# One loop in place of three on the path not taken, and its last stores on another queue

## Chip, cores and metric

The kernel runs on one core of a Trainium2 chip. The metric is the device time of one execution in microseconds, taken as the median of several runs. Besides, one execution was recorded by the profiler; all rows below are from it.

## What is computed

For each of 4 batches and 8 heads a gated linear attention runs over 768 time steps with a state of 48 x 48; its output, put together to 384 channels, goes through a causal convolution of 5 taps whose sigmoid gates a projection, and through a second projection:

```
for t in range(S):
    state = f[:, :, t, :, None] * state + einsum('bhd,bhe->bhde', k[:, :, t], v[:, :, t])
    y[:, :, t] = einsum('bhd,bhde->bhe', q[:, :, t], state)
...
gate = sigmoid(sum(conv_w[k] * xp[:, k:k + S] for k in range(5)))
out = (gate * (x @ w_val)) @ w_out
```

Here f is the sigmoid of the input f_logit, x is y with the heads side by side, and xp is x with four zero rows ahead of it.

## The kernel before

The kernel holds the computation twice. The **main path** (everything up to line 825) works in six chunks of 128 time steps. Within a chunk the recurrence becomes products of matrices, with running products of f factored into q and k. The order in which the five engines get their work is written out by hand in PROGRAM, a list of some hundreds of pieces; wrapped engines (class Ordered) keep that order. The chunked form is good only if the running products of f stay within a range. So the pieces rcheck, rcount and rflag form one number from the range test of all chunks, and the last of them writes `bad`.

At line 826 `values_load` brings `bad` into a register of each engine, and line 828 branches:

```
flag = nc.values_load(bad[:], min_val=0, max_val=1)
main.close()
with tc.If(flag == 0, preferred_fallthrough_block=False, label="good") as good:
    pass
with good.Else(), ExitStack() as sub:
    general(sub)
```

With a good flag nothing is left to do, and each engine jumps over the code of the **general path** (`general`, lines 636 to 711) to the closing barrier (line 883 of the builder). The general path would do the whole computation step by step with a scan: a nest of loops over the pairs of heads (two batch pairs `n`, four head pairs `i`, and `odd`; line 658) with an inner loop over the 48 rows of the state (line 675), and then a loop over the six chunks for convolution and projections (line 690). With the inputs of this kernel the flag is good, so none of it is executed; it only lies between the branch and the branch's target in each engine's instructions. SyncE issues the loads of q, f and k in it, ScalarE those of v and of the convolution's input and the stores of the pairs' results and of the outputs (lines 668, 689, 693, 711).

The pieces `hint 0` to `hint 4` (line 763) put one branch hint on each engine some time ahead of the branch, at places written in PROGRAM.

SyncE issues all stores of the main path (`send`, line 780); the last two pieces of its list are `send 6 2`, behind ScalarE's last copy, and the read of the flag.

The compiled program of the kernel before has 64 bytes for each instruction. Counted in it, labels of branch targets included (26 on each engine in this stretch), from the branch of line 828 to the first instruction of its target:

```
engine     instructions from branch to target     to the end of the program behind it
SyncE      221                                     22
ScalarE    193                                     6
VectorE    180                                     6
GpSimd     133                                     8
TensorE    274                                     6
```

## Time and profile before

| | |
|---|---|
| median of 3 runs | 191.07 us (191.02 to 191.68) |
| the profiled execution | 192.9 us |
| its span, first to last recorded instruction | 191.2 us |
| instructions recorded | 7637 |
| busy: TensorE, VectorE, ScalarE, GpSimd | 90%, 83%, 77%, 17% |
| last computing instruction ends | 184.7 us |

The profiled execution is 1.8 us above the median of the others; times within it are counted from the start of its span. The page's busy shares are means over the whole span. Register, branch, semaphore and DMA-issuing instructions are not counted as busy, so the stretch behind 184.7 us, in which there is nothing else, shows up in the page only as the zeros at the end of its slices. It is read from the instructions by line of the source: line 826 is the flag's read, line 828 the branch and the first instructions at its target, line 883 the closing barrier. In such rows "first and last start" is the place in time; a letter q behind an engine's name marks what its sequencer does itself (PEldq is TensorE's).

### The profile page before, as it was taken

What the parts mean: (1) busy time and instruction counts of PE and PEld (TensorE: products, weight loads), DVE (VectorE), ACT (ScalarE), POOL (GpSimd) and SP (SyncE); (2) the same over time, 40 slices, a digit from 0 to 9 for tenths busy, and PEclk for the clock granted to TensorE, in tenths of its full rate; (3) what the DMA queues carried; (4) which work ended last, traced back from release to release, by engine and by line L of the source; (5) the groups of instructions that cost most, each with busy time, mean ns of one, the idle gap of its engine ahead of it and who ended that gap; (6) DMA issues with size and microseconds to landing.
All of it is one profiled execution on the core that took longest, in us unless ns stands there. A gap on an engine that the chain in (4) does not pass through costs nothing.

```text
span 191.2 us, 7637 instructions
## 1 busy us (share of the span) xinstructions
PE 171.3 (90%) x3357; PEld 141.3 (74%) x3357; DVE 159.0 (83%) x236; ACT 146.9 (77%) x260; POOL 31.8 (17%) x57
## 2 busy tenths in 40 slices
PE   5478999996996899998999999989999999999960
PEld 1377878374885688887888887868878778898950
DVE  4069899999899999999999998999988989877000
ACT  8399799998775998987999999957357694575420
POOL 8300230088353300210000301200200000000000
PEclk9997999999999999999999999999999999999995
DMA  4997888887079648356389980620600010211430
GB/s 125 349 398 256 295 292 308 290 269 285 15 271 313 205 156 285 100 175 209 127 279 299 299 265 36 161 93 5 206 3 3 7 55 0 110 56 57 165 118 7
DMA packets 13064, 33.21 MB, mean 174 GB/s; under 512 B 1632, under 2 KB 3680, under 8 KB 13024
## 3 DMA queue, kind: packets, MB, share of 16 engines
q1 hardware_dynamic: 13024, 32.66, 50.5%
q8 instruction: 27, 0.44, 1.0%
q14 instruction: 13, 0.11, 0.2%
HBM read 26.75 MB, written 4.72 MB: 165 GB/s over the span
## 4 chain that ended last, share of the span: by engine, by line
PE 52%; DVE 22%; ACT 8%; DMA 6%; issue 4%; POOL 4%; SPq 1%; DVEq 0%
PE psum L127 52%; DVE kb L127 4%; DVE gt L127 4%; ACT e L127 4%; POOL wvL L127 4%; DMA qb<-in_q 3%; DVE qb L127 3%; DMA e<-in_f 3%; DVE e L127 2%; DVE asb L127 2%; DVE xL L127 2%; DVE ca L127 2%; DVE cb L127 1%; ACT ksb L127 1%; ACT xf L127 1%
## 5 line engine op out<-in xcount | busy, mean ns | idle before, releaser
L127 ACT ACTIVATE e<-e 128x1024 f32<-128x1024 f32 (+2 forms) x54 | 50.3, 942 | 3.6 <-DMA e<-in_f 3.0
L127 DVE SCALAR_TENSOR_TENSOR gt<-xf,cws,gt 128x512 f32<-128x512 f32 x48 | 37.4, 804 | 0.3 <-ACT gt L127 0.2
L127 PE MATMUL psum<-rg,woH 128*128 128x512 f32 (+1 forms) x108 | 32.1, 382 | 0.2 <-issue 0.2
L127 PE MATMUL psum<-asb,vb 64*32 64x64 f32 (+3 forms) x1152 | 27.5, 246 | 0.5 <-issue 0.4
L127 PEld LDWEIGHTS psum<-asb,vb 64*32 64x32 f32 (+1 forms) x1152 | 23.5, 115 | 1.7 <-issue 0.8
L127 DVE TENSOR_TENSOR_SCAN e<-keep,e 128x1024 f32<-128x1024 bf16 x10 | 23.9, 2386 | 0.0
L127 PE MATMUL psum<-qb,kb 64*64 64x128 f32 (+1 forms) x768 | 19.8, 250 | 2.8 <-DVE qb L127 2.4
L127 PEld LDWEIGHTS psum<-rg,woH 128*128 128x128 f32 x108 | 19.2, 188 | 3.8
L127 ACT CAST rg<-psum 128x512 fp32r<-128x512 f32 x30 | 17.1, 601 | 5.9 <-DVE psum L127 3.1
L127 PEld LDWEIGHTS psum<-qb,kb 64*64 64x64 f32 x768 | 17.9, 136 | 4.8 <-DVE qb L127 3.1
L127 PE MATMUL psum<-rg,woL 128*128 128x512 f32 (+1 forms) x54 | 20.3, 376 | 0.0
L127 PE MATMUL psum<-xH,wvL 128*128 128x512 f32 x45 | 17.9, 398 | 1.6 <-POOL wvL L127 1.6
L127 PE MATMUL psum<-xH,wvH 128*128 128x512 f32 x45 | 18.6, 414 | 0.6 <-DVE asb L127 0.5
L127 PE MATMUL psum<-qb,st 64*32 64x128 f32 (+1 forms) x480 | 19.1, 282 | 0.0
L127 PE MATMUL psum<-xL,wvH 128*128 128x512 f32 x45 | 17.8, 396 | 0.8 <-DVE xL L127 0.8
L127 DVE TENSOR_TENSOR kb<-kb,e 128x512 f32<-128x512 f32 (+1 forms) x28 | 17.2, 655 | 0.6 <-ACT e L127 0.6
L127 DVE TENSOR_TENSOR qb<-qb,e 128x1024 f32<-128x1024 f32 (+1 forms) x14 | 15.7, 1122 | 0.8 <-DMA qb<-in_q 0.8
L127 DVE TENSOR_TENSOR asb<-psum,tri 128x512 f32<-128x512 f32 x24 | 16.2, 681 | 0.0
L127 ACT COPY osb<-psum 128x512 f32<-128x512 f32 x15 | 8.6, 594 | 6.6 <-PE psum L127 6.5
L127 POOL TENSOR_TENSOR st<-u,e 128x384 f32<-128x384 f32 x8 | 9.2, 1157 | 26.0 <-DVE u L127 11.1
L127 PE MATMUL psum<-vb,ksb 128*64 128x48 f32 x320 | 11.6, 225 | 1.7 <-ACT ksb L127 1.7
L127 ACT COPY xf<-psum 128x768 f32<-128x768 f32 x12 | 9.6, 813 | 4.4 <-PE psum L127 4.4
(92 smaller groups left out, 309.0 us busy)
## 6 DMA issues: line engine op xcount, KB each, us to landing
e<-in_f SPq DMA_DIRECT2D x10, 512.0 KB, 5.7
kb<-in_k SPq DMA_DIRECT2D x10, 512.0 KB, 5.0
qb<-in_q SPq DMA_DIRECT2D x10, 512.0 KB, 5.2
vb<-in_v SPq DMA_DIRECT2D x10, 448.0 KB, 4.7
out<-osb SPq DMA_DIRECT2D x15, 256.0 KB, 3.7
raww<-in_wv SPq DMA_DIRECT2D x3, 384.0 KB, 4.9
raww<-in_wo SPq DMA_DIRECT2D x3, 384.0 KB, 5.8
e<-in_f SPq DMA_DIRECT2D x4, 256.0 KB, 4.6
```

Source lines behind the costliest of these rows:

```text
L127: ins = emit(*a, **kw)
```

## The change

The three loops over n, i and odd become one loop over all 16 pairs, and the indices are recovered from its counter by remainder and division. The three stores at the end of the loop over chunks are issued by SyncE instead of ScalarE. The main path is not edited.

```
-        with tc.For_i(0, 2, 1) as n, tc.For_i(0, NP, 1) as i, tc.For_i(0, 2, 1) as odd:
-            p = i * 2 + odd
-            bp = n * (2 * NP) + p
-            n1 = bass.ds(n, 1)
+        with tc.For_i(0, B * NP, 1) as bp:
+            p, odd = bp % (2 * NP), bp % 2
+            n1 = bass.ds(bp // (2 * NP), 1)
...
-                nc.scalar.dma_start(out[bass.ds(c, 1), :, o].rearrange("u p b t -> (u p) (b t)"), buf)
+                nc.sync.dma_start(out[bass.ds(c, 1), :, o].rearrange("u p b t -> (u p) (b t)"), buf)
```

## Rows read from the trace of the kernel before

**Rows 1.** The page's DMA queues: packets, MB, share of 16 engines' span.

```profile
q14 instruction: 13, 0.11, 0.2%
```

**Rows 2.** Busy time by stretch: PE, PEld, DVE, ACT, POOL, clock, DMA share, GB/s.

```profile
184.70:191.20 6.50, 0.00 (x0) 0.00 (x0) 0.00 (x0) 0.00 (x0) 0.00 (x0) 0.69 0.10 32
```

**Rows 3.** Line 828: operation, count, ns min/median/max, first and last start.

```profile
L828 SPq EVENT_SEMAPHORE  x8: 17/17/17, 189.3 to 189.8; - x8
L828 ACTq COMPARE_BRANCH  x1: 68/68/68, 184.9 to 184.9; - x1
L828 POOLq COMPARE_BRANCH  x1: 65/65/65, 184.9 to 184.9; - x1
L828 PEldq COMPARE_BRANCH  x1: 385/385/385, 185.0 to 185.0; - x1
L828 DVEq COMPARE_BRANCH  x1: 84/84/84, 185.0 to 185.0; - x1
L828 PEldq EVENT_SEMAPHORE  x1: 51/51/51, 185.4 to 185.4; - x1
L828 SPq COMPARE_BRANCH  x1: 70/70/70, 185.8 to 185.8; - x1
L828 ACTq EVENT_SEMAPHORE  x1: 17/17/17, 188.1 to 188.1; - x1
L828 DVEq EVENT_SEMAPHORE  x1: 21/21/21, 188.9 to 188.9; - x1
```

**Rows 4.** Line 883: the closing barrier, and the first of five hints.

```profile
L883 POOLq DRAIN  x3: 39/82/106, 185.4 to 190.9; - x3
L883 SPq DRAIN  x3: 7/7/7, 190.4 to 190.7; - x3
...
L883 POOLq BRANCH_PREFETCH_HINT  x1: 46/46/46, 147.1 to 147.1; - x1
```

**Rows 5.** SyncE's waits from 180 us: us in total, times, longest.

```profile
SPq L828 <- SPq L828: 3.4, 1, 3.4
```

**Rows 6.** DMA issues from 183 us: count, KB each, median us to landing.

```profile
out<-kb SPq DMA_DIRECT2D x2, 128.0 KB, 1.7
```

**Rows 7.** Instruction packets: 131 to 185.5, 185.9 to 186.1, 187.0 to 187.2, 188.7 to 189.9 us.

```profile
q8 instruction: 6, 0.10, 0.9%
...
q14 instruction: 3, 0.02, 36.0%
...
q14 instruction: 1, 0.01, 9.6%
...
q14 instruction: 3, 0.02, 6.4%
```

**Rows 8.** Instruction packets: 71.8 to 72.0 us, then 129.1 to 129.3 us.

```profile
q14 instruction: 1, 0.01, 17.2%
...
q14 instruction: 1, 0.01, 12.5%
```

**Rows 9.** Timeline of SyncE near 70 us: start, us, what.

```profile
70.20 0.42 SPq L127 DMA_DIRECT2D vb<-in_v  x1
```

**Rows 10.** SyncE's main line, 70.7 to 185.9 us: three of nine rows.

```profile
L127 SPq EVENT_SEMAPHORE  x34: 17/17/4687, 73.4 to 183.8; - x34
...
L127 SPq DMA_DIRECT2D out<-kb x6: 332/333/405, 179.2 to 184.5; - x6
...
L127 SPq DMA_DIRECT2D e<-in_f x2: 328/355/382, 91.5 to 101.8; - x2
```

**Rows 11.** ScalarE's main line, 107.2 to 185.0 us: first and last of 18.

```profile
L127 ACT CAST rg<-psum x18: 581/596/652, 113.8 to 168.5; 128x512 fp32r<-128x512 f32 x18
...
L127 ACT ACTIVATION_READ_ACCUMULATOR e<-e x1: 188/188/188, 113.4 to 113.4; 128x1 f32 x1
```

**Rows 12.** VectorE's main line, 128.2 to 185.1 us: first and last of 19.

```profile
L127 DVE SCALAR_TENSOR_TENSOR e<-xf,cws,e x24: 472/479/486, 152.7 to 171.4; 128x256 f32<-128x256 f32 x24
...
L127 DVE TENSOR_SCALAR bad<-psum x1: 145/145/145, 184.2 to 184.2; 1x1 int32<-1x1 f32 x1
```

## The prediction

> **What bounds the kernel now.** TensorE has most of the chain of waits, but nothing in it can be touched by this diff: the main path's order is written out by hand ahead of the branch, and the edited lines lie behind it, in a loop nest that these inputs do not run. What they can move is the end of the span and the transfers of instructions. So I read the page's DMA queues first: q14 carries instructions, 13 packets with 0.11 MB, about 8 KB each [rows 1]. An instruction of the compiled program is 64 bytes; a q14 packet is 128 of them.

> Then the busy time by stretch: from 184.7 us on no engine computes, and 6.5 us are left [rows 2]. That is the flag's read, the branch, the jump and the closing barrier.

> The view that decides the case is the branch's line [rows 3], with the closing line [rows 4]. ScalarE, GpSimd, TensorE and VectorE branch at 184.9 to 185.0, SyncE at 185.8, and all jump over the general path. TensorE's first instruction behind the jump stands at 185.4, 0.4 us after its branch began; GpSimd's at 185.4, 0.5 us after. ScalarE's stands at 188.1 (3.2 us), VectorE's at 188.9 (3.9 us), SyncE's at 189.3 (3.5 us). The wait view names SyncE's gap as the longest of the end, 3.4 us in which it waited for nothing but itself [rows 5]. It is no wait for data: the last store, issued at 184.5 [rows 10], lands within 1.7 us [rows 6], by 186.2. SyncE then works off its semaphore instructions, drains at 190.4, last of all, and the span ends 0.8 us later [rows 4].

> What fills the gaps is transfers of instructions. From 131 to 185.5 us the only instruction packets are six of q8, 16 KB each, while all five branch hints were executed from 147.1 on; then q14 has three packets within 185.9 to 186.1, one near 187.1 and three from 188.7 to 189.9 [rows 4, 7]. So the hints fetched nothing. The packets near 186.0 and 187.1 come 1.0 to 1.3 us behind the branches. TensorE alone runs through thousands of instructions: q8 is its queue, q14 that of the four others.

> **Where the blocks' edges lie.** Ahead of the branch q14 has packets near 71.9 and 129.2 [rows 8] and two like them, near 94.7 and 108.2. I read each as an engine that crosses into a new block and asks for the one behind it, 1.0 to 1.2 us ahead of the packet. At 70.6 SyncE ended a DMA issue and moved on [rows 9]; near 93.6 I take GpSimd, near 107.2 ScalarE, near 128.2 VectorE. From there I count instructions up to the branch. SyncE has 78 in nine rows [rows 10], and hint, read, two register instructions and branch: its branch is the 83rd of its block. ScalarE has 118 in 18 rows [rows 11] and three more, at most 121. VectorE has 87 in 19 rows [rows 12] and three more less the one in progress, at most 89. "At most", as a sequencer may run ahead of its engine.

> If the block behind the current one is always resident, a jump is free while offset plus distance stays under 256. The distances are those of the compiled program before (table in the section on the kernel). SyncE: 83 + 221 = 304, too far. ScalarE: 121 + 193 = 314, too far. VectorE: 89 + 180 = 269, just too far. GpSimd, some 22 instructions into its block, comes to 155: resident. All four agree with who waited. Without the 26 labels VectorE would be at 243 and should not have waited, so I count them.

> **The change, part by part.** One loop level costs in that program a block that skips it, one that resets semaphores, the head of the body, a block at its exit, and the step with its branch: 42 instructions on SyncE, 27 on ScalarE, 26 on VectorE and GpSimd. Two levels go. Nothing of it is executed, so its own time is zero before and after.

> Remainder and division are register operations; the program already packs up to seven into one instruction ahead of each DMA. They may add 0 to 4 instructions on SyncE and 0 to 3 on ScalarE; I take 0, as multiplications by the outer counters fall away, and keep the ends.

> The three moved stores are three DMAs with three address computations, three bound checks and two semaphore waits: 11 instructions off ScalarE. SyncE gets these and one move of the loop counter: 12. They do not run either, so no queue sees them; what SyncE's queue carries on the main path stays.

> New distances: SyncE 221 - 84 + 12 = 149, so 83 + 149 = 232. ScalarE 193 - 54 - 11 = 128, so at most 249. VectorE 180 - 52 = 128, so at most 217. All are under 256: the three targets come to lie in the next block, and three fetches leave the end. GpSimd's jump gets shorter and TensorE's too; both were free.

> The sum goes by SyncE, last before and last still: it branches 0.8 us behind the others. Its jump takes 3.5 us now [rows 3]. A resident jump takes 0.4 us on TensorE, 0.5 on GpSimd [rows 3, 4]; on SyncE it is not shown. Bounds: 0 us and 1.0 us (twice the slower row); I take 0.5. Gain 3.5 - 0.5 = **3.0 us**. What the gap had covered: ScalarE and VectorE now arrive by 185.6 and the last store by 186.2, both ahead of SyncE's target at 186.3, so neither is late next. The tail behind the target stays 1.9 us (189.3 to 191.2). The span becomes 188.2, the profiled execution 192.9 - 3.0 = 189.9. The median of the runs shown, 191.07, lies 1.8 below the profiled execution; the same 3.0 comes off it: **188.1 us**.

> [...]

> **Rivals.** *An edge in the tail* (20%). SyncE's target stands at 232, and with 21 more slots its last stands at 253, three short of the edge. Three added instructions, or what the runtime appends behind the program's own, cross it. The block behind is asked for only when the jump enters the one before, at 185.8, and by SyncE's own 3.5 us is usable at 189.3. Then the end is 189.3 plus between 0.3 and the barrier's 0.8: a gain of 1.1 to 1.6 us, 189.5 to 190.0 us. For it: the thin margin. Against it: only the last few instructions would be caught.

> *One of the two others still fetches* (9%). ScalarE's margin is 7 at the least, and added register instructions eat into it. It would arrive at 188.2; with the barrier's 0.8 us the span is 189.0, gain 2.2: 188.9 us. With VectorE at 189.0: gain 1.4, 189.7 us.

> *Nothing changes* (14%). SyncE's gap stays, since the blocks are not those that I read from the packets, or the gap hangs on something else than distance; the two other gaps are hidden behind it as now: 191.07 us. Against it: TensorE and GpSimd jump over the same path without a gap. [...]

> *Slower* (5%). SyncE still fetches its target, and this lands in the last 22 slots of its block: a second fetch follows the first. It is asked for on entry, 189.3 at the latest, and by the same 3.5 us is there at 192.8; with the barrier's 0.8 us the end is 193.6, 2.4 us later than now: 193.5 us. It decides from an offset plus distance of 363 to 383. Before that was 304 and the count only falls, so my edges would have to be off by 130 or so.

> **How the numbers follow.** The forecast has 52%, the rivals 20, 9, 14 and 5. A measurement of this kernel can tell about 0.5%, 0.96 us. Forecast, the edge and the one left fetch are all faster by more: 81%. Nothing changes is 14%, slower 5%. The range: below, a jump that costs nothing, 191.07 - 3.5 = 187.6; above, the worst of the edge, 190.0. That leaves out 19%.

> **What would show it.** On the branch's line SyncE's first semaphore instruction at about 186.3 instead of 189.3, ScalarE's and VectorE's at 185.4 to 185.6. The wait view's 3.4 us of SyncE gone. Still single q14 packets near 186, as entering a block asks for the next one, but nobody behind them. Everything ahead of 184.7 as it was. Wrong would be a SyncE gap of about 3 us in front of its target, or inside the closing instructions, which is the edge; and if ScalarE's and VectorE's gaps are gone at an equal span, my count of SyncE is off.

## The result and the profile after

The changed kernel takes 188.67 us (median of 4 runs, 188.44 to 189.52), the kernel before, measured beside it, 191.31 us (4 runs, 191.02 to 191.68). The ratio is 0.987, with a 95% interval of 0.983 to 0.991: faster by 1.8 to 3.2 us. The profiled execution took 188.44 us, its span 186.7.

The branch's line of the changed kernel, which answers to [rows 3] (operation, count, ns min/median/max, first and last start in us; the edit is one line shorter, so the line is now 827):

```profile
L827 SPq EVENT_SEMAPHORE  x8: 17/17/17, 184.8 to 185.3; - x8
L827 ACTq COMPARE_BRANCH  x1: 68/68/68, 183.4 to 183.4; - x1
...
L827 DVEq COMPARE_BRANCH  x1: 84/84/84, 183.5 to 183.5; - x1
L827 ACTq EVENT_SEMAPHORE  x1: 17/17/17, 183.9 to 183.9; - x1
...
L827 DVEq EVENT_SEMAPHORE  x1: 21/21/21, 184.1 to 184.1; - x1
L827 SPq COMPARE_BRANCH  x1: 70/70/70, 184.3 to 184.3; - x1
```

Read the pairs: ScalarE goes from branch to target in 0.5 us (3.2 before), VectorE in 0.6 (3.9), SyncE in 0.5 (3.5). The closing line shows the same tail as [rows 4], only earlier, with 0.8 us from SyncE's drain to the end of the span:

```profile
L882 POOLq DRAIN  x3: 39/45/82, 183.6 to 186.4; - x3
L882 SPq DRAIN  x3: 7/7/7, 185.9 to 186.2; - x3
```

In the wait view SyncE's wait for itself is down from 3.4 us [rows 5]:

```profile
SPq L827 <- SPq L827: 0.5, 1, 0.5
```

And q14 (packets, MB, share) still moves packets behind the branches, two within 184.6 to 184.9 us and one within 185.3 to 185.8, where [rows 7] had seven. No engine's gap goes with these three:

```profile
q14 instruction: 2, 0.02, 15.5%
...
q14 instruction: 1, 0.01, 4.3%
```

One caution for the two spans: they differ by 4.5 us, not by 3. The flag is written at 184.2 in the profiled execution of before [rows 12] and at 182.7 in that of after:

```profile
L127 DVE TENSOR_SCALAR bad<-psum x1: 146/146/146, 182.7 to 182.7; 1x1 int32<-1x1 f32 x1
```

These 1.5 us lie on the main path. Across the executions below, whose main paths hold the same work, the flag is written anywhere from 181.8 to 184.7 us, with either form of the loops; what moves it was not followed up. So the measure for everything that follows is the **end stretch**, from the start of the flag's write to the end of the span, taken from the records in nanoseconds: 6.98 us before, 4.04 after, 2.94 us less.

### The profile page after: what moved, and what is told of

Its sections match the earlier page's. It is cut to its first block, busy times and chain, and to the rows that moved or that the text cites. A ratio compares the mean times of both kernels' runs of the same rounds, so it can differ in the third digit from the quotient of the medians.

```text
span 186.7 us, 7638 instructions
## 1 busy us (share of the span) xinstructions
PE 170.6 (91%) x3356; PEld 141.1 (76%) x3357; DVE 158.8 (85%) x236; ACT 147.2 (79%) x260; POOL 34.1 (18%) x57
## 4 chain that ended last, share of the span: by engine, by line
PE 50%; DVE 27%; ACT 6%; DMA 6%; POOL 4%; issue 4%; SPq 1%; DVEq 0%
PE psum L127 50%; DVE kb L127 5%; DVE e L127 5%; DVE gt L127 4%; POOL wvL L127 4%; DVE qb L127 4%; DMA qb<-in_q 3%; ACT e L127 3%; DMA e<-in_f 3%; DVE asb L127 2%; DVE xL L127 2%; DVE ca L127 2%; DVE cb L127 1%; DVE u L127 1%; ACT xf L127 1%
## 5 line engine op out<-in xcount | busy, mean ns | idle before, releaser
L127 PE MATMUL psum<-qb,kb 64*64 64x128 f32 (+1 forms) x768 | 20.8, 257 | 2.6 <-DVE qb L127 2.0
L127 PEld LDWEIGHTS psum<-qb,kb 64*64 64x64 f32 x768 | 19.0, 141 | 4.7 <-DVE qb L127 2.6
L127 POOL TENSOR_TENSOR st<-u,e 128x384 f32<-128x384 f32 x8 | 10.1, 1262 | 25.6 <-DVE u L127 11.1
```

Of the source, the lines that this page charges most:

```text
L127: ins = emit(*a, **kw)
```

## The experiments

| run | SyncE's, ScalarE's, VectorE's gap, us | end stretch, us |
|---|---|---|
| before | 3.48, 3.24, 3.91 | 6.98 |
| after | 0.53, 0.47, 0.60 | 4.04 |
| stores_alone | 3.48, 2.99, 4.05 | 6.98 |
| loops_alone | 0.53, 2.64, 0.60 | 4.25 |
| two_loops | 2.86, 3.10, 0.61 | 6.37 |
| no_hints | 0.52, 0.45, 0.57 | 4.02 |
| old_padded | 0.52, 0.47, 0.61 | 4.01 |
| shift_25 | 2.97, 0.47, 0.60 | 6.48 |
| shift_50 | 0.52, 0.47, 0.60 | 4.03 |
| sp_tail | 2.89, 0.47, 0.60 | 6.41 |
| sp_target | 2.97, 0.47, 0.60 | 6.48 |
| va_near | 0.53, 0.47, 0.60 | 4.04 |
| va_far | 0.53, 3.02, 3.36 | 5.19 |
| last_on_act | 0.53, 0.49, 0.60 | 3.54 |

A gap is from the start of an engine's branch to its first instruction behind the jump. Each row is one execution; where no ratio is given below, the run has no other. The five with nothing but free jumps and SyncE last (after, no_hints, old_padded, shift_50, va_near) lie within 4.01 to 4.04 us, so a tenth of a microsecond in the end stretch is no scatter.

**The change in its parts.** Only the stores moved, the three loops kept:

```
-                nc.scalar.dma_start(out[bass.ds(c, 1), :, o].rearrange("u p b t -> (u p) (b t)"), buf)
+                nc.sync.dma_start(out[bass.ds(c, 1), :, o].rearrange("u p b t -> (u p) (b t)"), buf)
```

> Three loops kept, the three stores moved to SyncE. Measure: from the start of the flag's write (VectorE's last instruction) to the end of the span, 7.0 us in the kernel before, 4.0 in the changed one. Blocks theory (a jump is free while the branch's offset in its block plus the distance is under 256): SyncE 85 + 233 = 318, ScalarE at most 121 + 183 = 304, VectorE at most 89 + 180 = 269, so all three still fetch, SyncE's gap 3.5 us, 7.0 us to the end, time as before (191.3 us, within 0.5%). Rival, that ScalarE's stores themselves mattered: some of the 2.6 us gained.

Ratio to the kernel before 1.003 (0.9997 to 1.006), gaps as before. The stores alone give nothing. Then the loops alone, with the stores left on ScalarE:

> One loop, the stores left on ScalarE: SyncE 83 + 137 = 220, VectorE at most 89 + 128 = 217, ScalarE at most 121 + 138 = 259, or less by as much as its sequencer ran ahead. Blocks theory: SyncE and VectorE free; ScalarE within three of the edge. If it fetches, its gap is 3.2 us and the end comes 4.8 us after the flag's write instead of 4.0, and the moved stores are worth 0.8 us; if not, 4.0 us and the moved stores are worth nothing. Rival, that only the loops' code counts: 4.0 us.

ScalarE fetches, as the only engine, and in less time than expected (the branch's line of that run):

```profile
L827 ACTq COMPARE_BRANCH  x1: 68/68/68, 182.7 to 182.7; - x1
...
L827 SPq COMPARE_BRANCH  x1: 70/70/70, 183.6 to 183.6; - x1
L827 ACTq EVENT_SEMAPHORE  x1: 17/17/17, 185.4 to 185.4; - x1
```

2.64 us from branch to target, in nanoseconds. It arrives while SyncE's tail runs and holds it up by 0.2 us: the end stretch is 4.25 us. So the loops are worth 2.7 of the 2.9 us and the moved stores the last 0.2: they take ScalarE from a distance of 138, with its gap of 2.64 us, to 128, with 0.47. Two loops instead of one:

```
-        with tc.For_i(0, B * NP, 1) as bp:
-            p, odd = bp % (2 * NP), bp % 2
-            n1 = bass.ds(bp // (2 * NP), 1)
+        with tc.For_i(0, B * NP // 2, 1) as i, tc.For_i(0, 2, 1) as odd:
+            p = (i % NP) * 2 + odd
+            bp = i * 2 + odd
+            n1 = bass.ds(i // NP, 1)
```

> Two loops (pairs of pairs, and odd), stores on SyncE: one loop level less than before instead of two. Blocks theory: SyncE 85 + 193 = 278 and ScalarE at most 121 + 155 = 276 fetch, VectorE at most 89 + 154 = 243 does not. So VectorE's gap is 0.6 us, SyncE's 3.5 us, and the end stays 7.0 us after the flag's write: nothing gained. Rival, the gain goes with the length of the code: about half, 5.5 us.

VectorE is free, SyncE and ScalarE are not, as expected engine by engine. The end stretch is 6.37, not 7.0, since SyncE's fetch took 2.9 us instead of 3.5. It is no half of the gain. Nor does a shorter jump explain the shorter fetch: with at most one other engine fetching, SyncE's takes 2.9 to 3.0 us at distances of 193, 179, 159 and 149 (this run, sp_target, sp_tail, shift_25). Of VectorE's own gap 3.3 us are gone (3.91 to 0.61) and have bought nothing by themselves, as SyncE is last, its target at 187.4 us and VectorE's at 184.3.

**Place, not length.** If the edge of such a block decides, instructions ahead of the branch must be able to cure the kernel before:

```
+        "pad": lambda e, n: [(PE, DVE, ACT, POOL, SP)[e].drain(fusable=False) for _ in range(n)],
...
-mrest 6 0; mrest 5 2; hint 1; mrest 6 2; mrest 5 1; mhigh 6 1; send 4 0; mout 5 2; mstore 4 1; mstore 4 2; mrest 6 1;
+mrest 6 0; mrest 5 2; hint 1; mrest 6 2; mrest 5 1; mhigh 6 1; pad 2 35; pad 4 50; send 4 0; mout 5 2; mstore 4 1; mstore 4 2; mrest 6 1;
...
-send 5 1; mout 6 2; rcount; mstore 6 0; busy 1; send 5 0; mstore 6 1; hint 4; send 6 0; send 6 1; mstore 6 2; hint 0;
+send 5 1; mout 6 2; pad 1 50; rcount; mstore 6 0; busy 1; send 5 0; mstore 6 1; hint 4; send 6 0; send 6 1; mstore 6 2; hint 0;
```

> The kernel before, with all three loops and ScalarE's stores, and drains added on the main path in idle time ahead of the flag: 50 on SyncE, 35 on ScalarE, 50 on VectorE. They move the branch in its block and leave the distance. Blocks theory: SyncE's offset becomes 133, that is 5 in the next block, 5 + 221 = 226; ScalarE 146 to 156, that is 18 to 28, at most 28 + 193 = 221; VectorE 131 to 139, that is 3 to 11, at most 11 + 180 = 191. All under 256: the three gaps fall to 0.5 us, 4.0 us from the flag's write to the end instead of 7.0, and the time falls by some 3 us (188.3 us) though the program got longer. Rival, the length of the code or the loops count, not the place: gaps of 3.2 to 3.9 us as before, 191.3 us or more.

It takes 188.82 us, ratio 0.987 (0.981 to 0.993), with all three loops and 135 instructions more. The branch's line of that run:

```profile
L828 SPq EVENT_SEMAPHORE  x8: 17/17/17, 184.9 to 185.4; - x8
L828 ACTq COMPARE_BRANCH  x1: 68/68/68, 183.5 to 183.5; - x1
...
L828 DVEq COMPARE_BRANCH  x1: 89/89/89, 183.6 to 183.6; - x1
L828 ACTq EVENT_SEMAPHORE  x1: 17/17/17, 184.0 to 184.0; - x1
...
L828 DVEq EVENT_SEMAPHORE  x1: 21/21/21, 184.2 to 184.2; - x1
L828 SPq COMPARE_BRANCH  x1: 70/70/70, 184.4 to 184.4; - x1
```

All three gaps are 0.5 to 0.6 us over a path as long as before. This is the run that refutes the length of the code as the cause. That the drains work by their place, and not as such, the next two runs show: the same in the changed kernel, with SyncE alone shifted:

```
-mrest 6 0; mrest 5 2; hint 1; mrest 6 2; mrest 5 1; mhigh 6 1; send 4 0; mout 5 2; mstore 4 1; mstore 4 2; mrest 6 1;
+mrest 6 0; mrest 5 2; hint 1; mrest 6 2; mrest 5 1; mhigh 6 1; pad 4 25; send 4 0; mout 5 2; mstore 4 1; mstore 4 2; mrest 6 1;
```

> The changed kernel, with 25 drains on SyncE's main path in idle time; the distance stays 149. Blocks theory: offset 85 + 25 = 110, 110 + 149 = 259, just over: SyncE's gap is back at 3.5 us, 7.0 us from the flag's write to the end. Rival, distance alone decides: gap 0.5 us, 4.0 us.

> The changed kernel, with 50 drains on SyncE's main path; the distance stays 149. Blocks theory: offset 135, that is 7 in the next block, 7 + 149 = 156: gap 0.5 us, 4.0 us from the flag's write to the end, so twice as many added instructions as in the run with 25 cost nothing. Rival, distance alone decides: the same as with 25. Rival, added instructions ahead of the branch delay it: worse than with 25.

The branch's lines of the two runs, with 25 drains and with 50. With 25 SyncE's branch stands at 185.2 and its target at 188.2; with 50, at 183.8 and 184.3:

```profile
L827 SPq EVENT_SEMAPHORE  x8: 17/17/17, 188.2 to 188.7; - x8
...
L827 SPq COMPARE_BRANCH  x1: 70/70/70, 185.2 to 185.2; - x1
```

```profile
L827 SPq EVENT_SEMAPHORE  x8: 17/17/17, 184.3 to 184.8; - x8
...
L827 SPq COMPARE_BRANCH  x1: 70/70/70, 183.8 to 183.8; - x1
```

The wait comes and goes with the place, at an unchanged distance of 149. Twice the added instructions cost nothing. With 25 SyncE's gap is shorter than expected (2.97 us for 3.5, so 6.48 for 7.0), as in every run in which SyncE fetches without both others.

Pauses ahead of the branch agree with blocks of 128. In all 14 executions SyncE pauses for 0.44 to 0.45 us behind its 79th recorded instruction, whatever that instruction is, and a q14 packet follows. In the changed kernel the pause lies between the two semaphore instructions of this line, 17 and 28 ns long (67.4 to 68.1 us):

```profile
L127 SPq EVENT_SEMAPHORE  x2: 17/22/28, 67.5 to 68.0; - x2
```

With 50 drains added to the changed kernel SyncE pauses again, for 0.34 us, behind its 207th instruction, 128 further on. The 208th is the hint, and a packet follows (first line: line 882; second: 180.5 to 180.7 us):

```profile
L882 SPq BRANCH_PREFETCH_HINT  x1: 60/60/60, 180.0 to 180.0; - x1
...
q14 instruction: 1, 0.01, 17.2%
```

I read each pause as the edge of a block. With 25 drains the branch is the 193rd instruction, ahead of the second edge, and from 131 us to it there is no q14 packet. The kernel before with drains on three engines has three in that time.

**Distance.** Instructions added on one engine to the path not taken, at its head, with the rest of the changed kernel as it is:

```
         dp = ctx.enter_context(tc.tile_pool(name="gdram", bufs=1, space=bass.MemoryType.DRAM))
...
+        for _ in range(30):
+            nc.sync.drain(fusable=False)
```

> The changed kernel with 30 more instructions on SyncE in the path not taken. Blocks theory: 85 + 179 = 264, over 256: SyncE's gap is 3.5 us, 7.0 us from the flag's write to the end, the other engines free. Rival, SyncE's gap was cured by something else than the distance: 0.5 us, 4.0 us.

The wait view of that run has the wait back:

```profile
SPq L829 <- SPq L829: 2.9, 1, 2.9
```

The same with 30 on VectorE and 4 on ScalarE, and with 50 and 20:

> The changed kernel with 30 more instructions on VectorE and 4 on ScalarE in the path not taken. Blocks theory: VectorE at most 89 + 158 = 247, ScalarE at most 121 + 132 = 253: both resident, gaps of 0.5 to 0.6 us, 4.0 us from the flag's write to the end.

> The changed kernel with 50 more instructions on VectorE and 20 on ScalarE in the path not taken. Blocks theory: VectorE 81 to 89 + 178 = 259 to 267, ScalarE 111 to 121 + 148 = 259 to 269: both fetch, VectorE's gap 3.9 us, ScalarE's 3.2 us, SyncE's still 0.5. VectorE is then last, and the end comes 5.5 us after the flag's write instead of 4.0.

Both as expected in who waits: nobody in the first, ScalarE (3.0 us) and VectorE (3.4 us) in the second, and SyncE in neither. VectorE's fetch was expected to take 3.9 us, so the end stretch is 5.2 us and not 5.5. The branch's line of the second:

```profile
L831 ACTq COMPARE_BRANCH  x1: 68/68/68, 182.5 to 182.5; - x1
...
L831 DVEq COMPARE_BRANCH  x1: 84/84/84, 182.6 to 182.6; - x1
...
L831 ACTq EVENT_SEMAPHORE  x1: 17/17/17, 185.5 to 185.5; - x1
L831 DVEq EVENT_SEMAPHORE  x1: 21/21/21, 185.9 to 185.9; - x1
```

The single totals of these two (190.11 and 188.70 us) stand the wrong way round. The flag was written at 184.3 in the first and at 181.8 in the second; the end stretch, 4.04 and 5.19 us, is what the edit changed.

**A miss.** With 10 on SyncE:

> The changed kernel with 10 more instructions on SyncE in the path not taken. Blocks theory: target at 85 + 159 = 244, resident, gap 0.5 us; but the last of the 22 closing instructions would stand at 265, so the edge at 256 lies 12 behind the target. The block behind it is asked for only at the jump: a stall inside the closing semaphore instructions until 3.0 to 3.5 us after the branch, and 5.8 to 6.3 us from the flag's write to the end. Rival, no edge (blocks read on ahead of time, or edges elsewhere): 4.0 us.

The end stretch (6.41 us) is near what was expected, the place is not. The stall stands in front of the target, not inside the closing instructions (the branch's line):

```profile
L829 SPq EVENT_SEMAPHORE  x8: 17/17/17, 188.5 to 189.0; - x8
...
L829 SPq COMPARE_BRANCH  x1: 70/70/70, 185.6 to 185.6; - x1
```

SyncE's target is free at a distance of 149 and not at 159. By my count of its offset, 85, and the estimate of 256, the edge should lie at 171. So by these two runs SyncE's edge is 12 to 21 instructions nearer than counted; the last section finds where most of that went.

**The hints** (all five pieces `hint` taken out of the list):

> The changed kernel without the five branch hints. Blocks theory: the hints fetch nothing, so 4.0 us from the flag's write to the end and gaps of 0.5 us. Rival, the changed kernel gains because a hint now finds its target near enough: gaps of 3 us and more come back, up to 7.0 us.

End stretch 4.02 us, gaps as in the changed kernel. The hints neither make nor spoil the changed kernel's gain.

**A version that goes further.** SyncE is last because its read of the flag begins behind its last store, in the changed kernel at 183.3 us, where the four others read it at 182.9:

```
-        SP.dma_start(oview(n, m) if n < last else oview(last, m, 2 * (n - last), 2 * (n - last) + 2), sbuf(n, m))
+        (ACT if (n, m) == (6, 2) else SP).dma_start(oview(n, m) if n < last else oview(last, m, 2 * (n - last), 2 * (n - last) + 2), sbuf(n, m))
```

> The changed kernel, with the last store of the main path issued by ScalarE, which made the data, instead of SyncE. SyncE is now last because its read of the flag begins 0.5 us behind the others', after that store. Theory: SyncE reads the flag with the others, reaches its target and the closing barrier 0.5 us earlier; ScalarE reads 0.4 us later, which its 2 us of slack cover; 3.5 us from the flag's write to the end, 188.2 us against 188.7. Rival, SyncE then waits for that store's landing, 1.7 us behind an issue as late as before: 3.8 to 4.0 us, nothing gained.

Now ScalarE reads the flag late and SyncE with the others (line 825):

```profile
L825 SPq TENSOR_LOAD <-bad x1: 479/479/479, 183.6 to 183.6; - x1
...
L825 ACTq TENSOR_LOAD <-bad x1: 481/481/481, 184.1 to 184.1; - x1
```

The end stretch is 3.54 us, 0.50 shorter, with the flag at 183.4 and the end at 186.9. In time: 188.32 us (6 runs, 187.78 to 188.90), ratio to the kernel before 0.982 (0.977 to 0.987), where the changed kernel had 0.987 (0.983 to 0.991). The intervals overlap, so in total time the half microsecond is not shown to be more than scatter; in the end stretch it is there.

## Why the prediction was right

*Where the time lies.* Right. Nothing on the main path had to change. The three gaps fell from 3.2 to 3.9 us to 0.5 to 0.6, and the end stretch by 2.94 us.

*Blocks and edges.* Right in kind for this kernel: in the two shifts SyncE's branch alone moves, at a distance of 149, and its gap is 2.97 and 0.52 us; in sp_target the distance alone grows, from 149 to 179, and the gap from 0.53 to 2.97. Old_padded, va_far and two_loops agree. SyncE's two pauses, behind its 79th and its 207th instruction, lie 128 apart, as the estimate from q14's packets had it. The forecasts for VectorE and ScalarE held in every run: VectorE is free at 158 and not at 178, ScalarE free at 132 and not at 138. The numbers behind them were off, and by luck it did not matter. The step from packets to offsets took a packet to follow an edge by 1.0 to 1.2 us; in the kernel before, the one near 71.9 follows SyncE's edge, the pause that ends at 69.7, by 2.1. So SyncE's branch is the 87th of its block there, not the 83rd. And the estimate of 256 for offset plus distance was too wide: in these counts 247 was free and 248 was not (last section). SyncE's target in the changed kernel, put at 232 of 256, stands at 238, ten below the first sum that fetched.

*Counting the parts.* The new distances came out as worked out, 149, 128 and 128, with nothing added by remainder and division. SyncE's two semaphore instructions ahead of the branch were not foreseen and cost two of its margin. That labels take slots is not shown, though the prediction leaned on it: without them the runs part at one sum as well (last section).

*The sum.* The predicted terms were a resident jump of 0.5 us (measured 0.53), a gain of 3.0 us (2.94 in the end stretch, 2.64 between the medians, inside an interval of 1.8 to 3.2) and 188.1 us (188.67). Of the 0.6 us between the last two, 0.24 are the median before, which came out at 191.31 in the comparison instead of the 191.07 from which the sum started, and 0.36 the smaller gain between the medians. The places forecast on the branch's line came some 1.5 us earlier than named, with the flag; the gaps are what was right in them.

*The rivals.* "Nothing changes" and "slower" did not come. "An edge in the tail" named the wrong place. The margin was thin indeed: ten more instructions bring the wait back (sp_tail), but in front of the target and not at the end of the tail. In the changed kernel the closing instructions pass without a stall (semaphores from 184.8 us, the last drain at 186.2), though by an edge so near they ought to cross it; the rival's stall inside them is shown by no run. *One of the others still fetches* was the nearest: loops_alone shows that it would have come without the moved stores, at a cost of 0.2 us of the gain where I had priced 0.8 (188.9 against 188.1 us), since ScalarE branches 0.9 us ahead of SyncE and its fetch, with no other beside it, took 2.6 us.

## What to carry to other kernels

Where a kernel ends in a branch over code that rarely runs, look at the first instruction behind the jump on every engine. On SyncE, ScalarE and VectorE it stood 0.45 to 0.61 us behind the branch here where the jump was free, and 2.64 to 4.05 us where it was not, with instruction packets beside it [rows 7] and nothing to wait for. In this kernel the two parted by the branch's place, counted from the engine's pause, plus the length of what is jumped over: 247 was free, 248 was not. Shortening the skipped code was one cure (end stretch 6.98 to 4.04 us); moving the branch on with cheap instructions in idle time, 35 to 50 drains on an engine in old_padded, was another, worth as much (6.98 to 4.01). To find that place, the engine's own pause served better, which on SyncE came at the same instruction in every run, than the packet, which followed it by 0.6 us after and by 2.1 before. What an engine that is not last loses hardly showed: ScalarE's 2.64 us in loops_alone cost 0.2 us of the end stretch. So free the engine that arrives last first, then look who is next.

## What the runs showed that I had not expected

*Three fetches side by side took longer.* SyncE's gap is 3.48 us when ScalarE and VectorE fetch too (before and stores_alone) and 2.86 to 2.97 in the four runs in which at most one other engine does. VectorE's is 3.91 and 4.05 with both others, 3.36 with ScalarE alone. ScalarE's alone is 2.64, in company 2.99 to 3.24. Each number is one execution, and what the fetches share was not tried.

*One sum for three engines.* Count the offsets from the edges that show themselves instead of from the packets. SyncE's pause makes its branch the 89th instruction of its block in the changed kernel and the 87th before. In old_padded the rows of drains, which start every 0.03 to 0.04 us, are interrupted once on ScalarE (0.31 us) and once on VectorE (0.40 us); taken as their edges, these make the branches the 115th and the 86th in either kernel without drains. Offset plus distance then reaches 247 at most where the jump is free (ScalarE in va_near; VectorE 244 there, SyncE 238 in the changed kernel) and 248 at least where it fetches (SyncE in sp_tail; ScalarE 253 in loops_alone, VectorE 264 in va_far). So SyncE's edge is no nearer than the others': in these counts all 14 executions part between 247 and 248, with nine instructions to spare for SyncE in the changed kernel. In place of "12 to 21 nearer than counted" that leaves eight to the estimate of 256, the same for all.

Why the runs part eight short of two blocks of 128 stays open. The distances count the labels as slots (26 in the kernel before, 16 in the changed one). Left out, they bring the first sum that fetched to 232, and the runs part there as well; so whether the loaded program holds them is not shown.

*The closing instructions.* By that sum the changed kernel's SyncE should cross an edge among them. They start at the same distances as in shift_50, within 0.02 us, where the target stands at 160 and no edge is near. Nothing like the 0.44 us of SyncE's earlier edge is there, and no run says why.
